# A fused attention and rational feed-forward kernel: first loads per head, a stored 1e-9 beside each row sum, and a new table of due times

## The chip, the cores and the metric

The kernel runs on one core of a Trainium2 chip. The metric is the device time of one execution in microseconds (us). TensorE (PE) multiplies matrices, VectorE (DVE), ScalarE (ACT) and GpSimd (POOL) work elementwise, and SyncE (SP) issues every DMA. Each engine runs its own instructions in the order in which the program lists them and waits, at the head of its queue, for what the next one needs.

## The reference, cut to what matters

```python
def rotate(x):                      # q, k: (4, 8, 576, 64); cos, sin by position
    x1, x2 = x[..., :half], x[..., half:]
    return np.concatenate([x1 * cos - x2 * sin, x1 * sin + x2 * cos], axis=-1)
scores = scale * np.matmul(rotate(q), rotate(k).transpose(0, 1, 3, 2))
attn = np.exp(scores - scores.max(-1, keepdims=True))
attn = attn / (np.sum(attn, axis=-1, keepdims=True) + 1e-09)
x = np.matmul(attn, v)              # then (2304 tokens, 512)
h = x @ w_in                        # 512 -> 2048
P = a[0] + a[1] * h + a[2] * h**2 + a[3] * h**3
Q = 1.0 + np.abs(b[0]) * np.abs(h) + np.abs(b[1]) * h**2
out = (P / (Q + 1e-6)) @ w_out      # 2048 -> 512
```

## The kernel before

The 32 heads are taken as 16 pairs (0 to 15). Every fp32 operand of a product is split into a high and a low half that TensorE takes as fp32r, so a product is two or three matmuls.

A pair goes through named steps, and the names are used below with the pair's number. `ld` loads q and k of both heads, each with a copy whose halves are swapped, so that the rotation is two products with a table (`ro0`, `ro1`) and a sum (`ro2`). `hi` and `lo` split the result, `kh`, `kl`, `qh`, `ql` move halves between partitions by DMA. `s0` to `s8` are nine blocks of 128 rows of scores (PSUM, two buffers), `m` their negated maxima (tiles `nm`), `x` the exponentials (tiles `e`), with the row sum written by the same instruction into `sum`. `tA`, `tB`, `tL`, `tJ` transpose e on TensorE (three PSUM buffers), `h..` and `l..` split that into `eh` and `el`, `av0` to `av3` multiply by v, `ac` and `aa` add the two halves of that (tiles `xt`, `xo`). `n0` makes 1/(sum + 1e-9) in the tile `rs`: a tensor_scalar that adds 1e-9 (L468), then a reciprocal (L469). `n1` to `n4` spread it over partitions by way of DRAM, and `f0`, `f1` scale and store the pair's rows. `vh` and `vl` split v.

POOL does `ro0`, `ro1`, `ro2`, `lo`, `vl` and `f0` of a pair. For pairs 0 and 1 the rotation and `lo` are on DVE (`rope_first`, `split_first`, and `SECOND`), because POOL's are slower. Pair 0 is loaded in four pieces (`load_first`), and its rotation has its own instructions per head.

The feed-forward part goes through 73 units, most of them 512 tokens by 128 columns of the hidden layer: `up` (tile `h`, 12 matmuls), a chain of 13 elementwise steps on ACT, DVE and POOL (`t` to `gl`; `u`, `v`, `p`, `gh`, `gl` are its tiles), and `down` (tiles `acc0` to `acc3`). Each of the 32 weight tiles comes as raw 64-bit numbers and is made fp32 by four steps `wn0` to `wn3` (ACT or POOL, then three on DVE: tiles `rawi`, `rawo`), then split by `whh` (ACT) and `whl` (POOL). `up` and `down` of a tile wait for its `whl`.

No loop writes the program's order. `Program.order` is a list scheduler at build time: it holds each step's engine, a planned duration and a due time, and at each point an engine takes, of the steps that could start soonest, the one with the earliest due time. Due times come from tables: `SLOTS` for a pair, tables of their own for pairs 0, 1, 14 and 15, multiples of `TURN`, and `DUE`, `DUE_0`, `DUE_1` for the rest. A step marked `shared` is planned not to overlap POOL's; `n0` is not marked.

```python
    def norm(self, p, i):
        if i == 0:
            rs = st["rs"] = self.p2.tile([P, NBLK], F32, tag="rs", name=f"rs{p}")
            nc.vector.tensor_scalar(rs, st["sum"], 1e-9, None, ALU.add)
            nc.vector.reciprocal(rs, rs)
```

Of the kernel before, what the change touches and what calls it, by code (L numbers as in the profile page):

```python
# [17 lines left out]
P = 128  # L18
# [13 lines left out]
def fp(ap):  # L32
    return ap.bitcast(F32)
# [16 lines left out]
}  # L50
SLOTS_14 = {
# [12 lines left out]
}  # L64
SLOTS_15 = {
# [12 lines left out]
}  # L78
SLOTS_1 = {
# [12 lines left out]
}  # L92
SLOTS_0 = {
# [1041 lines left out]
```

## Time and profile before

| | |
|---|---|
| three runs, median | 750.04 us (746.74 to 753.43) |
| the profiled execution | 749.95 us, of which 748.1 us is its span, first to last instruction |
| busy in the span | PE 92%, PE weight load 79%, DVE 81%, ACT 79%, POOL 60% |
| granted TensorE clock, mean | 0.974 of full |
| moved by DMA | 86.34 MB, 115 GB/s |

The span has five parts. Until about 44 us pair 0 is loaded, rotated and scored. From there to about 274 us the pairs follow each other, with the score block `s4` of a pair at 104.16 us and that of the next at 120.96 us. From 274 to 387 us the last two pairs and the first units of the feed-forward part are mixed. From 387 to about 735 us PE hardly idles, and the last 13 us finish the last unit. The share of an engine over the whole span mixes these parts, so the rows by stage say more. A busy PE is a PE with some matmul under way: its records overlap, so the step from one start to the next is what a matmul costs.

### The profile page before, as it was taken

To read this page: it belongs to the slowest core of one execution; us is meant where nothing else is said; L and a number is where in the kernel's file an instruction comes from. 1 tells how busy PE (TensorE), PEld (TensorE's weight loads), DVE (VectorE), ACT (ScalarE), POOL (GpSimd) and SP (SyncE) were. 2 spreads that over 40 slices of the span, in tenths; PEclk is the share of its full clock that TensorE was granted. 3 is DMA by queue.
4 is the path that set the end of the run, shared out by engine and by line. 5 is a ranking of instruction groups with operands and counts; after the bars stand their busy time and mean duration, and the time that the engine had idled before them with its cause. 6 is when DMAs were issued, how large, how long until landed. Compare 5 with 4: busy or idle time off the path is not lost.

```text
span 748.1 us, 11378 instructions
## 1 busy us (share of the span) xinstructions
PE 690.4 (92%) x3864; PEld 591.0 (79%) x3864; DVE 602.7 (81%) x941; ACT 588.5 (79%) x1110; POOL 449.5 (60%) x293
## 2 busy tenths in 40 slices
PE   5679999999999987688799999999999999999998
PEld 2668999998998976666587788888888888888986
DVE  4867999999999888989988999866866666666675
ACT  1468999999998977787878998877767777677774
POOL 0576788788887646368667676656544454444422
PEclk9599999999999999998899999999999999999999
DMA  9476676777775754363432425205200001000100
GB/s 234 132 197 164 177 201 178 192 191 199 199 209 153 190 149 154 122 186 110 170 111 85 141 85 197 72 1 169 91 1 1 0 8 56 1 1 0 43 15 29
DMA packets 35305, 86.34 MB, mean 115 GB/s; under 512 B 5024, under 2 KB 8240, under 8 KB 33328
## 3 DMA queue, kind: packets, MB, share of 16 engines
q1 hardware_dynamic: 35248, 85.62, 39.8%
q8 instruction: 31, 0.51, 0.3%
q14 instruction: 26, 0.21, 0.1%
HBM read 55.25 MB, written 12.66 MB: 91 GB/s over the span
## 4 chain that ended last, share of the span: by engine, by line
PE 73%; DVE 11%; DMA 5%; ACT 5%; issue 2%; POOL 2%; SPq 1%; POOLq 0%; ACTq 0%; DVEq 0%
PE h L810 25%; PE acc L860 9%; PE acc L859 9%; PE acc L858 9%; PE s L445 9%; PE av L533 7%; DVE nm L453 3%; PE t_B L503 2%; PE t_A L503 2%; DVE rs L468 2%; DMA q<-q 2%; ACT e L460 2%; ACT eh L520 1%; DVE el L522 1%; DMA x<-in_qk_dram 1%
## 5 line engine op out<-in xcount | busy, mean ns | idle before, releaser
L834 POOL TENSOR_TENSOR v<-v,t 128x512 f32<-128x512 f32 x68 | 88.5, 1301 | 98.0 <-ACT v L832 97.0
L445 PE MATMUL s<-ks,q 128*128 128x288 f32 (+2 forms) x672 | 121.1, 313 | 19.8 <-ACT e L460 11.7
L843 POOL TENSOR_TENSOR gl<-u,gh 128x512 fp32r<-128x512 f32 (+1 forms) x73 | 94.3, 1292 | 62.4 <-ACT gh L842 45.6
L460 ACT ACTIVATE e<-s,nm 128x576 f32<-128x576 f32 x144 | 106.4, 740 | 28.4 <-DVE nm L453 26.5
L445 PEld LDWEIGHTS s<-ks,q 128*128 128x128 f32 x672 | 98.9, 198 | 28.1 <-ACT e L460 17.7
L453 DVE TENSOR_REDUCE nm<-s 128x1 f32<-128x576 f32 x144 | 105.4, 746 | 16.7 <-PE s L445 12.8
L533 PE MATMUL av<-eh,vv 128*128 128x288 f32 x320 | 91.6, 310 | 7.5 <-DVE xo L550 7.5
L860 PE MATMUL acc<-woh,gl 128*128 128x512 f32 x234 | 92.4, 395 | 0.7 <-POOL gl L843 0.7
L858 PE MATMUL acc<-woh,gh 128*128 128x512 f32 x234 | 92.4, 395 | 0.3 <-ACT gh L842 0.3
L859 PE MATMUL acc<-wol,gh 128*128 128x512 f32 x234 | 92.4, 395 | 0.0
L533 PE MATMUL av<-el,vv 128*128 128x288 f32 x320 | 87.4, 297 | 0.2 <-DVE el L522 0.2
L831 ACT ACTIVATE t<-h 128x512 f32<-128x512 f32 (+1 forms) x73 | 43.2, 591 | 54.3 <-PE h L810 54.1
L835 DVE TENSOR_TENSOR u<-u,h 128x512 f32<-128x512 f32 (+1 forms) x73 | 49.5, 678 | 44.5 <-ACT u L833 44.4
L371 POOL TENSOR_TENSOR x<-x,tab 128x1152 f32<-128x1152 f32 x28 | 75.5, 2698 | 14.1 <-DMA x<-in_qk_dram 14.1
L839 DVE SCALAR_TENSOR_TENSOR v<-v,p 128x512 f32<-128x512 f32 (+1 forms) x73 | 49.5, 678 | 34.5 <-ACT p L838 32.2
L810 PE MATMUL h<-xh,wih 128*128 128x512 f32 (+1 forms) x204 | 75.1, 368 | 0.0
L810 PE MATMUL h<-xh,wil 128*128 128x512 f32 (+1 forms) x204 | 74.9, 367 | 0.0
L810 PE MATMUL h<-xl,wih 128*128 128x512 f32 (+1 forms) x204 | 74.7, 366 | 0.0
L533 PEld LDWEIGHTS av<-eh,vv 128*128 128x128 f32 x320 | 60.9, 190 | 9.8 <-DVE xo L550 6.9
L533 PEld LDWEIGHTS av<-el,vv 128*128 128x128 f32 x320 | 61.1, 191 | 0.4 <-DVE el L522 0.4
L832 ACT ACTIVATE v<-t,const 128x512 f32<-128x512 f32 (+1 forms) x73 | 59.1, 810 | 2.4 <-DVE p L840 0.5
L842 ACT ACTIVATE gh<-u 128x512 fp32r<-128x512 f32 (+1 forms) x73 | 45.4, 622 | 19.6 <-PE acc L859 16.9
(113 smaller groups left out, 1747.6 us busy)
## 6 DMA issues: line engine op xcount, KB each, us to landing
x<-in_qk_dram SPq DMA_DIRECT2D x15, 1152.0 KB, 7.9
ks<-q SPq DMA_DIRECT2D x30, 288.0 KB, 3.6
q<-q SPq DMA_DIRECT2D x30, 288.0 KB, 7.1
rawi<-in_w_in_dram SPq DMA_DIRECT2D x16, 512.0 KB, 4.0
rawo<-in_w_out_dram SPq DMA_DIRECT2D x16, 512.0 KB, 3.2
vf<-in_v_dram SPq DMA_DIRECT2D x16, 320.0 KB, 3.6
rb<-rd SPq DMA_DIRECT2D x32, 144.0 KB, 3.4
xd<-xo SPq DMA_DIRECT2D x16, 288.0 KB, 2.7
```

The lines of the kernel that those rows point to most:

```text
L371: eng.tensor_tensor(x[:, i], x[:, i], t, ALU.mult)
L445: nc.tensor.matmul(ps[:, half, x:x + k.shape[-1]], q, k, start=(i == 0), stop=(i == len(ops) - 1))
L453: self.nc.vector.tensor_reduce(nm, st["s", c][:, :, :HALF], AX.XY, ALU.max, negate=True)
L460: self.nc.scalar.activation(e.rearrange("p (a b) -> p a b", a=2), st["s", c][:, :, :HALF], AF.Exp, bias=st["nm", c], scale=1.0, accum_out= ...
L533: nc.tensor.matmul(po[:, :HALF], v, e, start=(i == 0), stop=(i == len(ops) - 1))
L810: self.nc.tensor.matmul(ph[:, i * n:(i + 1) * n], w[:, k * P:(k + 1) * P], x[:, :n], start=(j == 0), stop=(j == len(terms) - 1))
L832: "v": lambda: act(new("v"), d["t"], AF.Identity, bias=self.b[0], scale=self.b[1]),
L834: "w": lambda: (nc.gpsimd.tensor_tensor if u < POOL_W else tt)(d["v"], d["v"], d["t"], ALU.mult),
L843: "gl": lambda: (nc.gpsimd.tensor_tensor(new("gl", F32R), d["u"], fp(d["gh"]), ALU.subtract), self.g.update({u: (d["gh"], d["gl"])})),
L858: nc.tensor.matmul(acc, gh[:, c], hi, start=(first and i == 0), stop=False)
L859: nc.tensor.matmul(acc, gh[:, c], lo, start=False, stop=False)
L860: nc.tensor.matmul(acc, gl[:, c], hi, start=False, stop=(last and i == len(fs) - 1))
```

## The change

Four things change.

1. In DRAM and in SBUF a head's plain and swapped halves lie side by side: `np.stack([xt, sw], 3)` in place of `2`. `load_first` then reads one unbroken stretch for a head, twice as long as each of the two before, with the same number of DMAs and bytes. The rotation of the other pairs takes `x[:, :, i]` in place of `x[:, i]`: the same number of elements.
2. The table of cosines and sines comes in one DMA in place of two halves, and `ro0` of pair 0 waits for all of it.
3. The row sums live in two fixed tiles of 9 pairs of numbers, whose second numbers are 1e-9, written once. `n0` is now a tensor_reduce over each pair of numbers, in place of the tensor_scalar; the reciprocal stays.
4. All due times are new, with a few planned durations (`vh`, `x`, `ac`, `aa`). Every engine's order changes.

```diff
+        self.sums = [self.p3.tile([P, NBLK, 2], F32, tag=f"sum{i}", bufs=1, name=f"sum{i}") for i in range(2)]
+        for t in self.sums:
+            nc.gpsimd.memset(t, 1e-9)
...
-            self.nc.sync.dma_start(self.x0[r:r + D, 2 * k:2 * k + 2, h], self.qk[0][k * D:(k + 1) * D, :, h])
+            self.nc.sync.dma_start(self.x0[r:r + D, 2 * k + h], self.qk[0][k * D:(k + 1) * D, h])
...
-        self.nc.sync.dma_start(self.tab[:, i], self.tab_dram[:, i])
+        self.nc.sync.dma_start(self.tab, self.tab_dram)
...
-            bias=st["nm", c], scale=1.0, accum_out=st["sum"][:, c:c + 1])
+            bias=st["nm", c], scale=1.0, accum_out=st["sum"][:, c, :1])
...
-            nc.vector.tensor_scalar(rs, st["sum"], 1e-9, None, ALU.add)
+            nc.vector.tensor_reduce(rs, st["sum"], AX.X, ALU.add)
             nc.vector.reciprocal(rs, rs)
...
-TURN = 17.89
+TURN = 16.49
...
-    "down": 20.59, "flush": -44.65, "late": -4.20, "each": 1.75, "x": 339.04, "x0": -596.98, "wl": 489.52,
+    "flush": 39.75, "late": -57.11, "each": 2.71, "x": 158.07, "x0": -650.32, "wl": 152.63, "wn": 175.59,
...
-        return np.stack([xt, sw], 2)
+        return np.stack([xt, sw], 3)
```

Three places show what the new due times do on DVE. A row gives the line, the operation, the tile written and the tiles read; a tile's first number is its pair, or its weight tile.

The first is the start of the program on DVE. x0 and x1 are q and k of pairs 0 and 1, q20 and q21 their split forms, nm0_1 the first maximum. Before:

```order
L378 TENSOR_TENSOR x0_110<-x0_110,tab_95 128x576 x2
L380 TENSOR_TENSOR x0_110<-x0_110 128x576
L378 TENSOR_TENSOR x0_110<-x0_110,tab_95 128x576 x4
L380 TENSOR_TENSOR x0_110<-x0_110 128x576 x2
L396 TENSOR_TENSOR q20_99<-x0_110,q20_99 128x576 x2
L394 SCALAR_TENSOR_TENSOR ks0_147<-x0_110,ks0_147 64x576
L378 TENSOR_TENSOR x0_110<-x0_110,tab_95 128x576 x2
L453 TENSOR_REDUCE nm0_1_203<-s0_1_192 128x1
```

The same engine and place with the change:

```order
L379 TENSOR_TENSOR x1_119<-x1_119,tab_95 128x2x576 x2
L381 TENSOR_TENSOR x1_119<-x1_119 128x2x576
L386 TENSOR_TENSOR x0_114<-x0_114,tab_95 128x576 x2
L417 TENSOR_TENSOR q21_100<-x1_119,q21_100 128x2x576
L388 TENSOR_TENSOR x0_114<-x0_114 128x576
L386 TENSOR_TENSOR x0_114<-x0_114,tab_95 128x576 x3
L388 TENSOR_TENSOR x0_114<-x0_114 128x576
L386 TENSOR_TENSOR x0_114<-x0_114,tab_95 128x576
L388 TENSOR_TENSOR x0_114<-x0_114 128x576
L404 TENSOR_TENSOR q20_99<-x0_114,q20_99 128x576
```

Pair 1's four instructions, which stood between the maxima of pair 0, now stand ahead of most of pair 0's. Behind the last row shown come four more on x0 and ks0 and then nm0_1. Up to the first maximum of pair 1, nm1_1, the order before has six `el0` and `el4_0` rows (five of 512 columns, one of 64), the new one two of 512. SP issues the load of x1 first, then the table, then the eight pieces of x0; before it issued x1 after all of x0.

The second is the place of `n0` in the middle, here of pair 8, on DVE. xo7 and el8 are outputs of pair 7 and split transposes of pair 8, nm9 the maxima of pair 9. Before:

```order
L453 TENSOR_REDUCE nm9_1_2301<-s9_1_2286 128x1
L453 TENSOR_REDUCE nm9_3_2310<-s9_3_2296 128x1
L550 TENSOR_TENSOR xo7_2183<-av7_2_2268,xt7_2_2308 64x288
L468 TENSOR_SCALAR rs8_2328<-sum8_2071 128x9
L469 RECIPROCAL rs8_2328<-rs8_2328 128x9
L453 TENSOR_REDUCE nm9_2_2349<-s9_2_2331 128x1
L522 TENSOR_TENSOR el8_2198<-t8_B_1_2303,eh8_2196 128x512
```

With the change:

```order
L530 TENSOR_TENSOR el8_2184<-t8_A_0_2248,eh8_2182 128x512
L476 TENSOR_REDUCE rs8_2286<-sum0_107 128x9
L477 RECIPROCAL rs8_2286<-rs8_2286 128x9
L461 TENSOR_REDUCE nm9_1_2296<-s9_1_2281 128x1
L530 TENSOR_TENSOR el8_2184<-t8_A_1_2258,eh8_2182 128x512
L558 TENSOR_TENSOR xo7_2199<-av7_2_2265,xt7_2_2289 64x288
L461 TENSOR_REDUCE nm9_3_2320<-s9_3_2291 128x1
```

The division stands four rows earlier, ahead of pair 9's first maximum, and the maxima and the `el` rows alternate more. Apart from the one operation, the rows of a pair are the same in number and size.

The third is the end of the scores on DVE: the weight tiles' steps among the last maxima of pair 15. Before:

```order
L453 TENSOR_REDUCE nm15_6_4009<-s15_6_3989 128x1
L522 TENSOR_TENSOR el15_3941<-t15_A_0_3943,eh15_3939 128x512
L686 SCALAR_TENSOR_TENSOR rawi2_3806<-rawi2_3806 128x512
L690 TENSOR_SCALAR rawo0_3905<-rawo0_3905 128x512
L691 SCALAR_TENSOR_TENSOR rawo0_3905<-rawo0_3905 128x512
L550 TENSOR_TENSOR xo14_3965<-av14_2_4011,xt14_2_4039 64x288
L522 TENSOR_TENSOR el15_3941<-t15_A_1_3997,eh15_3939 128x512
L686 SCALAR_TENSOR_TENSOR rawo0_3905<-rawo0_3905 128x512
L690 TENSOR_SCALAR rawi3_4025<-rawi3_4025 128x512
L691 SCALAR_TENSOR_TENSOR rawi3_4025<-rawi3_4025 128x512
L453 TENSOR_REDUCE nm15_7_4075<-s15_7_4066 128x1
```

With the change:

```order
L461 TENSOR_REDUCE nm15_8_3989<-s15_8_3969 128x1
L530 TENSOR_TENSOR el14_3657<-t14_B_2_3940,eh14_3655 128x512
L530 TENSOR_TENSOR el15_3931<-t15_A_2_3933,eh15_3929 128x512
L558 TENSOR_TENSOR xo14_3959<-av14_1_3976,xt14_1_3994 64x288
L697 SCALAR_TENSOR_TENSOR rawi2_3807<-rawi2_3807 128x512
L692 SCALAR_TENSOR_TENSOR rawi2_3807<-rawi2_3807 128x512
L461 TENSOR_REDUCE nm15_7_4030<-s15_7_4011 128x1
```

The steps of rawo0 and rawi3 move behind the last maximum. Counted on DVE from pair 14's maximum nm14_4 to the last step `g` of unit 4, the order before has 129 rows, 42 of them weight steps, and the new one 112, with 30. To `g` of unit 8 it is 163 (57) and 149 (45), to `g` of unit 27 303 and 301. On PE, five `up` units stand ahead of the first `down` of unit 0 in the new order, four in the old one.

More of the change, by code (lines that the diff above doesn't have):

```diff
@@ L115 @@
 DUE = {
-    "ffn": 374.36, "t": 20.70, "v": 234.46, "w": -228.61, "u1": 810.56, "u2": 217.88, "ln": -365.32,
-    "u3": 29.76, "ex": -511.21, "e": -170.92, "r": 223.55, "g": -3.82, "gh": -173.95, "gl": -268.30,
-    "down": 20.59, "flush": -44.65, "late": -4.20, "each": 1.75, "x": 339.04, "x0": -596.98, "wl": 489.52,
-    "wn": -36.51, "wh": -35.53, "w0": -79.89, "w1": 10.51, "w2": 294.91, "w3": 394.40, "w4": 464.21,
-    "w5": -759.74, "w6": 263.05, "w7": 282.47, "x1": 170.86, "x1s": 25.55,
[5 rows of a table added]
 }
 DUE_0 = {
-    "t": 265.57, "v": 583.68, "w": -379.99, "u1": 354.36, "u2": -835.24, "ln": -198.44, "u3": 379.54,
-    "ex": -271.89, "e": -448.85, "r": 170.65, "g": 263.61, "gh": 5.48, "gl": -193.04, "down": 88.90,
-    "flush": -28.37,
+    "t": -7.80, "v": 396.31, "w": -9.41, "u1": 399.03, "u2": -351.99, "ln": -346.35, "u3": 427.36,
+    "ex": -358.45, "e": -342.95, "r": -56.25, "g": 416.20, "gh": 6.97, "gl": 446.65, "down": 388.26,
+    "flush": -36.80,
 }
 DUE_1 = {
-    "roq": -285.89, "rok": 0.41, "hiq": 81.20, "hik": -107.48, "loq": -46.08, "lok": -40.44,
+    "roq": -274.70, "rok": 447.98, "hiq": 438.00, "hik": 440.39, "loq": 463.53, "lok": -305.02,
 }
@@ L263, in attention_steps @@
         st[f"m{c}"] = "D", 0.665, [f"s{c}"]
-        st[f"x{c}"] = "A", 0.717, [f"m{c}"]
+        st[f"x{c}"] = "A", 0.74, [f"m{c}"]
     of = {f"{k}{j}": list(range(4) if k == "A" else range(5, 9)) for k in "AB" for j in range(4)}
@@ L272, in attention_steps @@
         st[f"av{i}"] = "P", 1.36, ["vl"] + ["l" + g for g in of if g.startswith(kinds)]
-        st[f"ac{i}"] = "A", 0.29, [f"av{i}"]
-        st[f"aa{i}"] = "D", 0.44 if i == 3 else 0.37, [f"ac{i}"]
+        st[f"ac{i}"] = "A", 0.43, [f"av{i}"]
+        st[f"aa{i}"] = "D", 0.5 if i == 3 else 0.42, [f"ac{i}"]
     avs, scores = [f"av{i}" for i in range(4)], [f"s{c}" for c in range(NBLK)]
@@ L348, in load_first, with load_table @@
         for r in (0, D):
-            self.nc.sync.dma_start(self.x0[r:r + D, 2 * k:2 * k + 2, h], self.qk[0][k * D:(k + 1) * D, :, h])
-    def load_table(self, i):
-        self.nc.sync.dma_start(self.tab[:, i], self.tab_dram[:, i])
+            self.nc.sync.dma_start(self.x0[r:r + D, 2 * k + h], self.qk[0][k * D:(k + 1) * D, h])
+    def load_table(self):
+        self.nc.sync.dma_start(self.tab, self.tab_dram)
     def warm(self):
@@ L370, in rope @@
             t = self.tab[:, i:i + 1, :].to_broadcast([P, 2, S])
-            eng.tensor_tensor(x[:, i], x[:, i], t, ALU.mult)
+            eng.tensor_tensor(x[:, :, i], x[:, :, i], t, ALU.mult)
         else:
-            eng.tensor_tensor(x[:, 0], x[:, 0], x[:, 1], ALU.add)
+            eng.tensor_tensor(x[:, :, 0], x[:, :, 0], x[:, :, 1], ALU.add)
     def rope_first(self, k, h, i, eng):
-        x = self.x0[:, 2 * k:2 * k + 2, h]
+        x = self.x0[:, 2 * k + h]
         if i < 2:
@@ L382, in split_first @@
     def split_first(self, k, h, lo, eng):
-        nc, st, x = self.nc, self.st[0], self.x0[:, 2 * k, h]
+        nc, st, x = self.nc, self.st[0], self.x0[:, 2 * k + h, 0]
         ks, q2 = self.stacks(0)
@@ L404, in split_hi @@
     def split_hi(self, p):
-        self.nc.scalar.activation(self.stacks(p)[1][:, 0, :, :S], self.st[p]["x"][:, 0], AF.Copy)
+        self.nc.scalar.activation(self.stacks(p)[1][:, 0, :, :S], self.st[p]["x"][:, :, 0], AF.Copy)
     def split_lo(self, p, eng=None):
         q2 = self.stacks(p)[1]
-        (eng or self.nc.gpsimd).tensor_tensor(q2[:, 1, :, :S], self.st[p]["x"][:, 0], fp(q2[:, 0, :, :S]), ALU.subtract)
+        (eng or self.nc.gpsimd).tensor_tensor(q2[:, 1, :, :S], self.st[p]["x"][:, :, 0], fp(q2[:, 0, :, :S]), ALU.subtract)
     def move_k(self, p, t):
@@ L457, in exp @@
         if "sum" not in st:
-            st["sum"] = self.p2.tile([P, NBLK], F32, tag="sum", name=f"sum{p}")
+            st["sum"] = self.sums[p % 2]
         e = self.e4 if c == 4 else self.e[:, self.slot(p, c % 5), c // 5]
@@ L633, in plan_first @@
             add(("warm", i), "P", 0.216, WARM_DUE + 0.01 * i, self.warm, ["ident"], [("v", [("warm", WARM - 1)])] if i == 0 else [])
-        add(("tab", 0), "S", 0.0, -90, lambda: self.load_table(0), [], size=(1, 0.75))
+        add("tab", "S", 0.0, -90, self.load_table, [], size=(1, 1.8))
         for h in range(2):
@@ L638, in plan_first @@
                 n = "qk"[k]
-                add(("ld", 0, n, h), "S", 0.0, -89 + 4 * h + 2 * k, lambda k=k, h=h: self.load_first(k, h), size=(2, 1.5))
-                if k == h == 0:
-                    add(("tab", 1), "S", 0.0, -88.5, lambda: self.load_table(1), size=(1, 0.75))
+                add(("ld", 0, n, h), "S", 0.0, -89 + 4 * h + 2 * k, lambda k=k, h=h: self.load_first(k, h), size=(2, 2.0))
                 self.prog.shared |= {(f"ro{i}", 0, n, h) for i in range(3)} | {("lo", 0, n, h)}
@@ L644, in plan_first @@
                     add((f"ro{i}", 0, n, h), e, 0.67 * f, DUE_1[f"ro{n}"] + 0.01 * i if h else 4 * k + i - 80, lambda k=k, h=h, i=i, eng=eng: self.rope_first(k, h, i, eng),
-                        [("ro1", 0, n, h)] if i == 2 else [("ld", 0, n, h), ("tab", i)] + [("ro0", 0, n, h)] * i)
+                        [("ro1", 0, n, h)] if i == 2 else [("ld", 0, n, h), "tab"] + [("ro0", 0, n, h)] * i)
                 add(("hi", 0, n, h), "A", 0.573 + 0.1 * k, DUE_1[f"hi{n}"] if h else -80, lambda k=k, h=h: self.split_first(k, h, 0, None), [("ro2", 0, n, h)])
```

132 rows, old and new, of tables (DUE, SLOTS, SLOTS_0, SLOTS_1) are left out of this document.

## The prediction

> **What bounds the kernel now.** I read the page's totals, then the busy time by stage, then the chain that ended last, then single rows. The stages come first. Columns: stretch, its length, busy us and count for PE, PE's weight load, DVE, ACT and POOL, then granted clock, DMA share and GB/s.
>
> ```profile
> span 748.1 us, 11378 instructions
> 15.00:30.00 15.00, 7.07 (x26) 6.25 (x26) 13.55 (x18) 6.50 (x12) 2.86 (x2) 0.56 0.45 171
> 100.00:150.00 50.00, 48.34 (x375) 46.18 (x375) 48.03 (x81) 46.63 (x107) 40.26 (x19) 1.00 0.73 199
> ...
> 500.00:550.00 50.00, 50.00 (x219) 40.76 (x218) 36.76 (x55) 38.04 (x60) 29.43 (x23) 1.00 0.30 98
> ...
> 274.39:300.00 25.61, 19.53 (x144) 17.74 (x144) 19.74 (x34) 19.38 (x44) 14.16 (x10) 1.00 0.54 169
> 300.00:320.00 20.00, 14.09 (x97) 12.43 (x96) 18.09 (x34) 15.02 (x33) 7.74 (x6) 1.00 0.41 133
> 320.00:341.80 21.80, 15.37 (x81) 11.76 (x79) 18.26 (x32) 19.95 (x35) 13.07 (x11) 0.99 0.49 149
> 341.80:365.00 23.20, 23.20 (x94) 19.38 (x94) 22.00 (x32) 17.22 (x29) 17.36 (x14) 0.87 0.44 152
> 365.00:386.60 21.60, 16.63 (x63) 13.24 (x62) 19.34 (x29) 17.45 (x29) 14.88 (x12) 0.84 0.39 135
> sum 112.21, PE 88.81 PEld 74.55 DVE 97.43 ACT 89.01 POOL 67.22; mean PE 17.76 PEld 14.91 DVE 19.49 ACT 17.80 POOL 13.44
> ```
>
> The feed-forward part (500 to 550) is full on PE, so no order makes it shorter. The pairs (100 to 150) are close to full on three engines at once. At the start, and in the 112.21 us where pairs and units mix, PE idles while DVE does not: there PE has 23.4 us idle (112.21 less 88.81), DVE 14.8. So three places can move: start, pairs, mix.
>
> The chain of one pair, with start, us and what ran:
>
> ```profile
> 52.62 2.03 PE s L445 x14
> ...
> 104.16 1.16 PE s L445 x10
> ...
> 107.24 0.11 PE rt L472
> 107.35 0.44 PE t_B L503 x4
> 107.79 0.53 PE s L445 x4
> ...
> 108.76 0.22 PE t_J L503 x2
> 108.98 1.33 PE av L533 x10
> ...
> 116.49 1.65 DVE rs L468
> ...
> 120.96 1.16 PE s L445 x10
> ...
> 274.39 1.16 PE s L445 x10
> ```
>
> A pair takes 16.80 us here (104.16 to 120.96). From pair 1's `s4` at 52.62 to pair 14's at 274.39 there are 13 of them in 221.8 us, 17.06 each. One link is odd: 1.65 us for nine numbers per partition. Its rows, and what POOL did then:
>
> ```profile
> L468 DVE TENSOR_SCALAR rs<-sum x16: 165/1641/2437, 46.2 to 323.6; 128x9 f32<-128x9 f32 x16
> ...
> 132.25 2.65 POOL L409 TENSOR_TENSOR q<-x,q 128x1152 fp32r<-128x1152 f32 x1 [1.46 <-ACT q L405]
> 133.29 1.64 DVE L468 TENSOR_SCALAR rs<-sum 128x9 f32<-128x9 f32 x1
> 134.97 0.22 DVE L469 RECIPROCAL rs<-rs 128x9 f32<-128x9 f32 x1
> ```
>
> The row ends at 134.93, with POOL's at 134.90. The least of the 16 takes 0.165, the median 1.641. So this tensor_scalar waits for POOL's instruction, while the reciprocal behind it takes 0.22 although POOL has begun again.
>
> **The pairs.** `n0`'s first row becomes a tensor_reduce of 18 numbers. No row here shows a reduce out of SBUF beside POOL. If it does not wait, it costs about 0.2, like the reciprocal; if it waits, 1.64 as before. I take 0.2, because the reciprocal, its nearest row, also reads SBUF and does not wait. That frees 1.44 us of DVE per pair. It is not all gain, since what is late next stands close. PE must issue, by the chain's rows, eight score blocks of 0.53 and one of 1.16, ten sets of four transposes at 0.44, one of 0.22, four `av` of 1.33 and `rt` 0.11: 15.45 us. ACT is busy 46.63 of 50, or 15.67 us per pair, and DVE falls from 16.14 to 14.7. So the gain is at most 16.80 less 15.67, 1.13 us by ACT, or 1.35 by PE's issue. At the least it is some 0.3, when the new order turns most of it into waits of ACT for maxima. I take 0.85, three quarters of ACT's bound. Over 13 pairs that is **11 us**, bounded by 4 and 17. The rest of the order in the pairs I cost at nothing: same rows, and POOL, at 40.26 of 50, covers its own waits; if that cover is gone, the lower bound holds.
>
> The Trainium skill, page SBUF — State Buffer, section Who interferes with whom, says the same of both operations: tensor_scalar may take a port pair that is an exclusive lock against GpSimd, and tensor_reduce on trn2 never contends. The first half is what the rows show; the second no run before can show. By it the sum above stands, and without it the case of the waiting reduce below.
>
> **The start.** Rows of before:
>
> ```profile
> 7.67 0.76 DVE L378 TENSOR_TENSOR x<-x,tab 128x576 f32<-128x576 f32 x1 [6.79 <-DMA x<-in_qk_dram]
> 13.88 1.43 DVE L378 TENSOR_TENSOR x<-x,tab 128x576 f32<-128x576 f32 x2 [1.14 <-DMA x<-in_qk_dram]
> 18.95 2.29 PE L445 MATMUL s<-ks,q 128*128 128x288 f32 x8 [5.96 <-DVE ks L394]
> 21.66 1.35 DVE L371 TENSOR_TENSOR x<-x,tab 128x1152 f32<-128x1152 f32 x1
> 21.11 0.74 ACT L460 ACTIVATE e<-s,nm 128x576 f32<-128x576 f32 x1 [0.16 <-DVE nm L453]
> 22.00 1.33 PE L445 MATMUL s<-ks,q 128*128 128x288 f32 x4 [0.76 <-ACT e L460]
> 28.39 1.17 ACT L405 ACTIVATE q<-x 128x1152 fp32r<-128x1152 f32 x1 [1.33 <-DVE x L373]
> 45.55 0.76 DVE L453 TENSOR_REDUCE nm<-s 128x1 f32<-128x576 f32 x1 [2.00 <-PE s L445]
> ...
> x<-in_qk_dram SPq DMA_DIRECT2D x8, 288.0 KB, 8.1
> tab<-in_tab_dram SPq DMA_DIRECT2D x2, 288.0 KB
> ```
>
> Between 7.67 and 13.88 five pieces of 288 KB came in (half the table and four of x0): 232 KB a us. The new order loads x1 first (1152 KB, being four times 288) and then the table: 864 KB have landed by 7.67, the other 864 take 3.7, so DVE starts at 11.4. Pair 0's four heads follow every 2.5 us, from 13.9 to 21.3, each ahead of its use. DVE: three rows of 1.35 on x1 to 15.5, two of 0.72 to 16.9, x1's `lo` (ACT's 1.17 is done by then) to 18.3, twelve rows of 0.72 to 26.9, then the first maximum. Thirteen such rows later, at 36.3, it reaches nm1_1, which stood at 45.55. Four more rows of `el` are still to be done then, three such and a small one, 2.3 us, so this way the new order is 7 us ahead: it no longer idles before data and `lo` of x1 is not stretched. But PE's first scores come at 25.6 rather than 18.95, after a longer idle, and a block of scores that comes after one takes 1.33, not 0.53. With two score buffers two blocks take 1.33, the maximum's 0.76 and the exponential's 0.74, so nine take 13 us. With 3.5 sets of transposes, 0.44 stretched alike to 1.1, and pair 1's first block, nm1_1 stands at about 43.8: then the gain is nothing. I take **3 us**, between, bounded by -2 (a wait for POOL at `lo`) and 7. The longer rows in DRAM and the one table DMA I cost at nothing: the bytes are the same, and x1 covers the table.
>
> A rule speaks against the later scores: the Trainium skill, page TensorE: Matmul & The Clock Gate, Part 1, says that an idle array is throttled to half rate until it has been busy for some 3.4 us. The stage rows agree on the fall (clock 0.56 from 15 to 30). By that rule dense scores would run at full rate after 3.4 us and the gain would be near 7; by the rows, where the clock stayed low through a stretch with 7.07 us of matmuls, it is the lower figure.
>
> **The mix.** The rows of DVE's weight steps (busy, then mean ns), two of PE's waits from 265 to 400, and all from 400 on (us in total, times, longest):
>
> ```profile
> L690 DVE TENSOR_SCALAR rawo<-rawo 128x512 int32<-128x512 int32 x16 | 10.5, 658 | 0.0
> L691 DVE SCALAR_TENSOR_TENSOR rawi<-wpi,rawi 128x512 int32<-128x512 int32 x12 | 8.3, 692 | 0.9
> ...
> PE av L533 <- DVE xo L550: 6.9, 6, 2.4
> PE h L810 <- DVE u L836: 5.6, 2, 5.0
> ...
> PE acc L860 <- POOL gl L843: 0.7, 1, 0.7
> PE acc L858 <- ACT gh L842: 0.3, 1, 0.3
> ```
>
> What PE waits for is DVE, twice over. To `g` of unit 8, near the end of this stretch, the new order has 14 fewer DVE rows, 12 of them weight steps. At 0.65 from start to start (0.69 less an overlap of about 0.04) they are 9.1 us. DVE is busy 97.43 of 112.21, so I let the whole come out of the stretch: **9 us**. The most is near 20, when PE's 23.4 idle us all but go and the clock (0.87 and 0.84) does not fall; the least -3, when other waits take their place. The steps come later, in units where PE is full and DVE at 36.76 of 50 has room. That cover hides them; where a tile comes after its unit it would cost up to 6 us, three tiles' steps.
>
> **Sum.** 749.95 (the profiled execution: the span and 1.85 around it) less 3, 11 and 9 is 726.95, so **727 us**. The median of the runs shown is 750.04, the same within 0.1.
>
> **The rivals.**
>
> The reduce waits like the tensor_scalar (the change then doesn't do what it says). For it: both read SBUF while POOL does; against it: the reciprocal. The 11 go: 749.95 less 12, 738.
>
> The new order gives it back. All three engines of a pair are above 46 of 50, and an order made for planned durations may meet other ones. At 0.3 us in a pair, and nothing at start and mix, it is 746.
>
> Weights come too late, which makes it slower than before. Twelve tiles' DVE steps stand later against the units, and PE waits for a tile in order. A tile's DVE steps take 2.04 us (0.66 and twice 0.69). If each of the 24 later tiles holds PE by three quarters of that, 1.5 us, that is 36, and 727 becomes 763. It decides from 1.3 us a tile (24 times 1.27 is the 23 gained and 1% more). Against it: PE lost 1.0 us to all waits after 400 (0.7 and 0.3), and nearly all `whl` rows stand more than a unit ahead.
>
> **How the numbers follow.** Forecast 0.72, the waiting reduce 0.07, given back 0.13, late weights 0.08. About 1% is what a measurement tells here, 742.5 to 757.5. The first two are faster, with a little of the third: faster 0.80, within 0.12, slower 0.08. The bounds of the terms, not all at one end, give 712 to 742 for the forecast; with part of the third case the range is 712 to 745.
>
> **What would show it.** L476 near 0.2 us in all 16; from `s4` to `s4` about 16 us; nm1_1 near 42; PE's idle time between `s4` of pair 14 and unit 9 down by 9 or more, and its clock full there; PE at 50 of 50 from 500 on. The forecast is wrong if L476 takes over 1 us, if ACT or PE waits in a pair grow by what DVE gained, or if `h` or `acc` wait for weights.

## The result, and the profile after

The changed kernel takes **720.37 us** (median of 4 runs, 719.73 to 722.84) against 750.49 for the kernel before in the same comparison (4 runs, 746.74 to 753.43): a ratio of 0.9607, 95% interval 0.9558 to 0.9656. The forecast was 727, in a range of 712 to 745. Medians and ranges below are of all runs, ratios and intervals leave out the runs of a slower state. The kernel before spreads: in three later comparisons its 17 to 29 runs had medians of 751.1 to 752.6. The profiled execution of the kernel with the new start alone is the longest of its 12 (760.51 against a median of 750.03), and only its first 65 us are read.

The profiled execution took 719.73 us, by the page:

```profile
span 718.0 us, 11373 instructions
```

The busy time by stage of the changed kernel, in the columns of the prediction (stretch, length, busy us of PE, its weight load, DVE, ACT and POOL, granted clock, DMA share, GB/s):

```profile
15.00:30.00 15.00, 5.93 (x21) 5.24 (x22) 12.58 (x18) 6.00 (x13) 4.38 (x3) 0.59 1.01 282
30.00:50.00 20.00, 18.26 (x131) 16.46 (x131) 16.34 (x28) 18.08 (x44) 14.43 (x6) 0.97 0.42 104
100.00:150.00 50.00, 48.46 (x380) 46.76 (x379) 44.76 (x83) 46.67 (x110) 40.78 (x19) 1.00 0.80 196
263.00:291.00 28.00, 24.84 (x183) 22.50 (x182) 25.91 (x46) 25.92 (x62) 16.88 (x12) 1.00 0.59 185
...
500.00:550.00 50.00, 50.00 (x219) 40.78 (x218) 34.71 (x50) 35.94 (x56) 23.86 (x19) 1.00 0.10 33
```

And two such rows of the kernel before, for the stretches that answer to the second and the fourth:

```profile
30.00:50.00 20.00, 14.71 (x77) 13.07 (x77) 14.31 (x20) 11.70 (x27) 16.51 (x6) 0.73 0.68 163
...
276.00:315.00 39.00, 27.79 (x202) 24.89 (x200) 32.15 (x56) 30.18 (x67) 17.33 (x13) 1.00 0.48 156
```

The feed-forward part is as full as it was. In the pairs PE is no fuller (48.46 of 50, before 48.34), although DVE has lost 3.27 us of work there. The start is denser from 30 us on, and what took 39 us around pair 15's maxima takes 28.

To place the gain, the rows of DVE were matched, line by line and in order, with the tiles that the program writes in that order. This gives the end of each event, in us. `nmP_B` is the maximum of block B of pair P, `u8` the last `u` of unit 8.

```
event      before   changed   lead        stretch that ends here   before   changed
nm1_1       46.30     38.15    8.2
nm2_4       71.52     63.59    7.9        start                     71.5      63.6
nm14_4     276.34    263.62   12.7        pairs                    204.8     200.0
nm15_7     315.04    291.61   23.4        mix, last two pairs       38.7      28.0
u8         392.20    361.90   30.3        mix, first units          77.2      70.3
last u     739.96    709.89   30.1        the rest                 347.8     348.0
```

So 7.9 us come from the start (forecast 3), 4.8 from the pairs (11), and 17.6 from the mix (9): 10.7 up to the last maximum and 6.9 behind it. Each number is of one execution. Two variants below have the changed kernel's order on every engine up to nm14_4, and in their traces the pairs take 202.4 and 202.2 us, not 200.0: 2 us in the pairs is what one execution differs from the next. Where a variant is named below, its numbers in such events are from its own trace in the same way.

### The profile page after: what moved, and what is told of

It reads as the page before. It is cut to its first block, busy times and chain, and to the rows that moved or that the text cites. A ratio compares the mean times of both kernels' runs of the same rounds, so it can differ in the third digit from the quotient of the medians.

```text
span 718.0 us, 11373 instructions
## 1 busy us (share of the span) xinstructions
PE 680.2 (95%) x3864; PEld 586.6 (82%) x3864; DVE 578.5 (81%) x941; ACT 584.9 (81%) x1110; POOL 447.8 (62%) x295
## 4 chain that ended last, share of the span: by engine, by line
PE 72%; DMA 14%; ACT 5%; DVE 5%; issue 1%; POOL 1%; SPq 1%; DVEq 0%; POOLq 0%; ACTq 0%
PE h L816 26%; PE acc L866 9%; PE acc L865 9%; PE acc L864 9%; PE s L453 7%; DMA ks<-q 7%; PE av L541 6%; DMA q<-q 4%; PE t_B L511 3%; ACT e L468 2%; PE t_A L511 2%; DMA const<-in_b_dram 1%; ACT eh L528 1%; PE t_J L511 1%; DMA tab<-in_tab_dram 1%
## 5 line engine op out<-in xcount | busy, mean ns | idle before, releaser
L461 DVE TENSOR_REDUCE nm<-s 128x1 f32<-128x576 f32 x144 | 107.9, 752 | 24.5 <-PE s L453 22.3
L453 PEld LDWEIGHTS s<-ks,q 128*128 128x128 f32 x672 | 97.0, 194 | 30.1 <-ACT e L468 11.2
```

The lines of the kernel that those rows point to most:

```text
L453: nc.tensor.matmul(ps[:, half, x:x + k.shape[-1]], q, k, start=(i == 0), stop=(i == len(ops) - 1))
L461: self.nc.vector.tensor_reduce(nm, st["s", c][:, :, :HALF], AX.XY, ALU.max, negate=True)
```

## The experiments

**The row sums, each way round.** One kernel is the changed one with the old row:

```diff
...
-            nc.vector.tensor_reduce(rs, st["sum"], AX.X, ALU.add)
+            nc.vector.tensor_scalar(rs, st["sum"], 1e-9, None, ALU.add)
```

> The changed kernel with n0's tensor_scalar and its own sum tile put back; order, loads and table stay. Theory A (the freed DVE time was not what the pairs of the new order gained, since q's copies by DMA set their step, 16.9 us before and after): the row takes about 1.6 us again in most pairs, DVE takes it out of its slack, and the kernel loses 2 to 8 us, 722 to 728. Rival B (the reduce is worth its 1.4 us in every pair): 13 times 1.3, 17 us, so 737.

The other is the kernel before with the new row and its fixed tiles:

```diff
...
-            nc.vector.tensor_scalar(rs, st["sum"], 1e-9, None, ALU.add)
+            nc.vector.tensor_reduce(rs, st["sum"], AX.X, ALU.add)
```

> The kernel before with only n0's tensor_reduce and the stored 1e-9; order, loads and table of before. Theory A (in the old order PE waited in the pairs for DVE and ACT and hardly for DMA): the row takes 0.16 us and the pairs fall from 16.8 towards 16.3, 4 to 8 us in all, 742 to 746. Rival B (other waits take its place at once): under 2 us, 748 to 750. Rival C (worth 0.85 a pair as the prediction had it): 739.

The first took 723.91 us (723.32 to 724.91; 0.9615 of before, 0.956 to 0.9669), the second 755.26 (751.67 to 760.46; 1.0035, 0.9997 to 1.0073). So in the new order the row is worth 3.5 us by the medians, but only 0.6 by the two ratios to the kernel before, whose intervals cover each other: a worth clear of noise is not shown. In the old order it is worth nothing that can be told; the second kernel came out above all three of its ranges, nearest to rival B. The row's durations (ns, least, median, most) in the changed kernel:

```profile
L476 DVE TENSOR_REDUCE rs<-sum x16: 150/153/174, 41.0 to 292.9; 128x9 f32<-128x18 f32 x16
```

The same row in the old order, in the second kernel:

```profile
L471 DVE TENSOR_REDUCE rs<-sum x16: 160/173/179, 45.5 to 334.2; 128x9 f32<-128x18 f32 x16
```

The old row in the new order:

```profile
L472 DVE TENSOR_SCALAR rs<-sum x16: 151/153/2190, 40.9 to 297.3; 128x9 f32<-128x9 f32 x16
```

The reduce never waits, as forecast. The second kernel is what shows it: a POOL row runs beside 15 of its 16 reduces, in the changed kernel beside 5, and beside none from pair 2 to pair 12. For the same reason the old row mostly does not wait in its new place: its median there is 0.153 us, where it was 1.641 in the old order. In pairs 2 to 12 both rows thus take 0.15 us, and what the reduce was to bring there the new place brings by itself. So the first kernel lies in theory A's range, but not in theory A's way, which had the old row wait again in most pairs. Where POOL does run, the old row still waits, here in pair 13, where POOL's row ends at 259.13:

```profile
257.16 2.00 DVE L472 TENSOR_SCALAR rs<-sum 128x9 f32<-128x9 f32 x1 [0.28 <-ACT e L464]
```

In the old order, 1.47 us less of DVE in a pair brought nothing. The chain of the second kernel in its middle (start, us, what) and two of POOL's waits from 60 to 250 us (total, times, longest) say what took over. The chain:

```profile
185.43 2.67 POOL q L412
...
188.11 4.26 DMA ks<-q
...
192.44 9.85 DMA q<-q
...
202.43 1.17 PE s L448 x7
```

POOL's waits:

```profile
POOL x L374 <- DMA x<-in_qk_dram: 20.4, 7, 5.3
POOL x L374 <- DMA vf<-in_v_dram: 11.0, 2, 5.7
```

From POOL's `lo` to the scores lie two transfers one after the other, 4.26 us for `kl` and 9.85 for `ql`; and POOL, which makes `lo`, waits for x. A pair first fell to 16.1 us, and from pair 7 on some took 18 to 21.5 us. DVE was not the only bound; the transfers behind POOL were as near. Two limits of this reading: the profiled execution is the longest of ten (760.46 against a median of 755.26), and the same chain stands, with the old row, in the profile of the kernel with only the new layout (3.49 us and 8.65 from 242.04 on). So the transfers belong to the old order and not to the reduce; how often a usual execution meets them is open.

**Where x's load stands on SP.** In the changed kernel's pairs one wait of PE stands out. Its longest from 41 to 235 us:

```profile
PE s L453 <- DMA q<-q: 7.4, 8, 1.6
```

The longest of the kernel before, from 52 to 265:

```profile
PE t_B L503 <- DVE el L522: 4.7, 10, 1.2
PE s L445 <- ACT e L460: 4.1, 12, 1.4
PE s L445 <- DMA q<-q: 0.8, 1, 0.8
```

PE no longer waits for DVE and ACT, but for `q`. The chain that ended last, in the changed kernel, from 105 us:

```profile
110.73 0.34 SPq L352
...
111.12 8.31 DMA ks<-q
...
119.44 0.02 SPq L425
...
119.49 3.79 DMA q<-q
...
123.41 1.16 PE s L453 x7
```

SP issues the load of x (L352, 1152 KB) and right behind it `kl` (288 KB), which takes 8.31 us to land. `ql` is issued when `kl` has landed (119.49, the row behind it in the chain), and PE's scores wait for `ql`. In the old order the load of x stood behind `kl` and ahead of `qh` and `ql`. Two kernels move it in pairs 2 to 13, all else as in the changed kernel: one behind `kl`, the other behind `ql`.

```diff
+    return {("ld", p + 2): at["kl", p] + 0.5 for p in range(2, 14)}
```

> The changed kernel with one DMA moved in SP's order for pairs 2 to 13: the load of x of the pair after next stands behind the second copy to ks (kl), where before it stood, not between kh and kl. Theory A (x's 1152 KB ahead of kl make kl land after 8 us, ql waits for kl and PE for ql): kl lands in about 4 us, PE's waits for q (7.4 us) go, the pairs fall from 16.7 to about 16.2, and the kernel gains 3 to 6 us, 714 to 717. Rival B (the DMA engines, 0.8 busy, set the step whatever the order): under 1 us, 719 to 721.

```diff
+    return {("ld", p + 2): at["ql", p] + 0.5 for p in range(2, 14)}
```

> The same with the load of x behind the last copy of q (ql), so that no copy of a pair has x's load ahead of it. Theory A: PE's waits for q go as well and the time is that of the run with x behind kl or 1 us less, 713 to 716, unless x then comes too late for POOL's first product (POOL waits for x over 5 us in all). Rival B: 719 to 721.

They took 714.60 us (712.34 to 716.60; 0.949 of before, 0.9451 to 0.9528), as theory A had it, and **711.33** (710.94 to 712.64; 0.9451, 0.9414 to 0.9488), 1.7 below its range, both faster than the changed kernel, whose interval (0.9558 to 0.9656) theirs do not touch. The median time to land of `ks` and `q`, by the page's part on DMA issues, in the changed kernel:

```profile
ks<-q SPq DMA_DIRECT2D x30, 288.0 KB, 5.7
q<-q SPq DMA_DIRECT2D x30, 288.0 KB, 4.6
```

The same in the second kernel:

```profile
ks<-q SPq DMA_DIRECT2D x30, 288.0 KB, 3.6
q<-q SPq DMA_DIRECT2D x30, 288.0 KB, 3.9
```

Of PE's waits for `q`, 7.4 us in the changed kernel, this is left there from 41 to 235 us:

```profile
PE s L480 <- DMA q<-q: 1.3, 1, 1.3
```

And its busy time from 100 to 150 us, in the columns above:

```profile
100.00:150.00 50.00, 49.55 (x393) 48.21 (x392) 46.44 (x86) 47.97 (x113) 42.29 (x20) 1.00 0.75 209
```

From nm2_4 to nm14_4 it takes 194.3 us where the changed kernel takes 200.0: 16.2 a pair, against 16.7 and 17.1 before, and 11 of its 12 pairs take 16.0 to 16.1. So the place of one load on SP's queue held back 5.7 of the 11 us that the prediction had for the pairs. Another 1.9 us are won ahead of nm2_4, since the edit begins with pair 2. The Trainium skill, page DMA: Bandwidth & Descriptors, section Queues, rings and completion order, says that on each DMA engine the descriptors of one queue are consumed in ring order. The rows agree: `kl` took 8.31 us behind x's load, and the median to land of `ks` is 3.6 without it ahead. In the kernel with x behind `kl` it is q's copies that have the load ahead of them, and there their median is 6.2 and that of `ks` 3.3.

**The start.** The layout and the one table load by themselves, in the kernel before:

```diff
...
-        self.nc.sync.dma_start(self.tab[:, i], self.tab_dram[:, i])
+        self.nc.sync.dma_start(self.tab, self.tab_dram)
...
-        return np.stack([xt, sw], 2)
+        return np.stack([xt, sw], 3)
```

> The kernel before with only the new layout: x of a head holds its plain and swapped half side by side, each first load is one unbroken piece of rows, and the table comes in one load. The order of the steps is the old one. Theory A (the layout is worth nothing, the gain at the start is the new order's): within 2 us of before, table and x landed no earlier than in before (7.67 and 6.79+ us after the start), nm1_1 at 45.5 +- 1. Rival B (longer rows in DRAM make the loads quicker): nm1_1 2 to 4 us earlier and the kernel 2 to 4 us faster, with the first loads landing sooner after their issue than 8.1 us.

It took 757.00 us (746.67 to 762.17; 1.0031, 0.9988 to 1.0074), no difference that can be told; nm1_1 stood at 45.86. The 7 us that its profiled execution lies behind arise at pairs 11 to 14, not at the start. Then the kernel before with the first loads and DVE's first rows in the new order, and pair 1's copies earlier on SP:

```diff
...
+    to = {("ld", 1): -1.0, ("tab", 0): -0.9, ("tab", 1): -0.8, ("lo", 1): second + 0.5}
+    to.update({(n, 1): first - 0.5 + 0.1 * i for i, n in enumerate(("ro0", "ro1", "ro2", "hi"))})
...
```

> The kernel before with only the start in the new order: x of pair 1 loaded first, its rotation and split ahead of pair 0's on VectorE, and its copies into the stacks earlier on SyncE. Layout, row sums and all later places are the old ones. Theory A (the place of pair 1's rotation makes the start shorter, and what is won there stays): nm1_1 at 38 to 40 us (before 45.55), nm2_4 7 to 8 us earlier than 71.52, the kernel 6 to 8 us faster (742 to 744). Rival B (the pairs of the old order give it back, since x of the pairs after comes no earlier): nm2_4 5 us or more earlier, but nm14_4 less than 2 us earlier than 276.3, and the kernel within 2 us of before.

It took 751.49 us (747.26 to 764.88; 0.9984, 0.9945 to 1.0022), with nm1_1 at 46.23. Neither theory had this: the lead did not even arise. PE's rows there, with the wait of each in brackets:

```profile
40.09 0.63 PE L535 MATMUL t_A<-ident,e 128*128 128x128 f32 x4 [0.78 <-DVE el L554]
...
42.32 0.97 PE L535 MATMUL t_J<-ident,e 128*128 128x128 f32 x4 [1.07 <-DVE el L554]
44.27 0.63 PE L535 MATMUL t_L<-ident,e 128*128 128x128 f32 x4 [0.98 <-DVE el L554]
44.65 0.79 PE L477 MATMUL s<-ks,q 128*128 128x288 f32 x4
```

The same place in the changed kernel:

```profile
35.50 0.81 PE L453 MATMUL s<-ks,q 128*128 128x288 f32 x4 [0.84 <-ACT e L468]
36.14 0.60 PE L511 MATMUL t_A<-ident,e 128*128 128x128 f32 x4
36.50 0.78 PE L453 MATMUL s<-ks,q 128*128 128x288 f32 x4
37.12 0.60 PE L511 MATMUL t_A<-ident,e 128*128 128x128 f32 x4
38.20 0.80 PE L453 MATMUL s<-ks,q 128*128 128x288 f32 x4 [0.49 <-ACT e L468]
```

With PE's old order, pair 1's first block (44.65) stands behind transposes of pair 0 that wait one after another for `el`; in the changed kernel it stands at 36.50, among them. The block itself waits for nothing at 44.65, and SP had issued pair 1's last copy of q by 22.54 there. So a third kernel takes the whole new order, on all engines, up to pair 2's `m4`, and the old one from there:

```diff
+    head = new[:new.index(("m4", 2)) + 1]
+    return head + [n for n in order if n not in set(head)]
```

> The kernel before (its layout, its tensor_scalar row), with the changed kernel's order on all engines up to pair 2's maximum m4 and its own from there on. Before, nm1_1 stood at 46.3 and nm2_4 at 71.5; in the changed kernel at 38.2 and 63.6; moving VectorE's and SyncE's rows alone had left nm1_1 at 46.2. Theory A (what shortens the start is that TensorE takes pair 1's scores between pair 0's transposes): nm1_1 at 38 to 40, nm2_4 at 63 to 66, and the kernel 5 to 8 us faster (743 to 746). Rival B (the old order of the pairs gives the lead back, waiting for x): nm2_4 as in A, but nm14_4 within 2 us of 276.3, and the kernel within 2 us of before.

nm1_1 came to 39.14 and nm2_4 to 64.50, as theory A had it, but the kernel took 750.03 us (744.39 to 760.51; 0.9958, 0.992 to 0.9995). A lead of 7 us ends as 3, between theory A and rival B. So the new order makes the start without the new layout. That it is PE's part of the order is read from the rows above: this kernel moves ACT's and POOL's rows too. Half of the lead or more is given back behind nm2_4; where, and whether by waiting for x as rival B had it, is not shown, as the one trace is of the longest execution. In the changed kernel, and in the one with only the row put back, nm2_4's lead of 7.9 us stands at 12.7 and 10.1 by nm14_4.

**The pairs alone.** The kernel before with the new order only between those two places:

```diff
+    mid = [n for n in new[:new.index(("m4", 14)) + 1] if n not in set(head)]
+    return head + mid + [n for n in order if n not in set(head + mid)]
```

> The kernel before (its layout, its tensor_scalar row), with the changed kernel's order between pair 2's maximum m4 and pair 14's, and its own start and end. From nm2_4 to nm14_4 before took 204.8 us, the changed kernel 200.0, and the changed kernel with the old row 202.7. Theory A (the new order of the pairs is hardly better in itself, since q's copy comes late behind x's load): 202 to 204 us, the kernel 0 to 3 us faster. Rival B (the new order of the pairs is worth what the changed kernel shows and more with a shorter start taken away): under 201 us, and the kernel 4 us or more faster.

It took 749.18 us (747.07 to 752.21; 0.9982, 0.9956 to 1.0008), and 205.9 us from nm2_4 to nm14_4, a little over what theory A named; its conclusion holds. Five of the 12 pairs take 16.0 to 16.1 us, the others 16.9 to 19.8. Alone, the new order of the pairs is worth nothing that can be told.

**The mix.** First the changed kernel with six weight rows put back ahead of pair 15's last maximum:

```diff
+    last = at["m7", 15]
+    steps = [(f"wn{i}", *w) for w in (("o", 0), ("i", 3)) for i in range(4)]
+    return {n: last - 0.9 + 0.1 * i for i, n in enumerate(steps)}
```

> The changed kernel with two weight tiles' rounding steps (six VectorE rows and their first steps) put ahead of pair 15's last maximum, where the old order has them. Theory A (in the mix every VectorE row costs its length, some 0.65 us): nm15_7 at 295 to 296 us instead of 291.6, and the kernel 3 to 4 us slower (724). Rival B (VectorE has room there): nm15_7 within 1 us, and the kernel within 1 us of the changed one.

It took 728.32 us (727.04 to 731.48; 0.9664, 0.9623 to 0.9705): 8 over the changed kernel by the medians, more than theory A, and 4 by the two ratios. Its profiled execution is the longest of its six (731.48). Up to nm14_4, where the order is the changed kernel's row for row on every engine, it was already 4.1 us late, with 10.0 us of PE's waits for `q` against 7.4; this part is not the edit's, and why those transfers took longer in that comparison stays open. From nm14_4 to the last `u` it takes 453.9 us, the changed kernel 446.3: the edit costs 7.6 in this execution, or 1.3 us a row, twice a row's own length; by the ratios it would be 0.7. DVE at that place:

```profile
299.10 1.66 DVE L721 SCALAR_TENSOR_TENSOR rawi<-rawi 128x512 int32<-128x512 int32 x1
300.68 0.74 DVE L490 TENSOR_REDUCE nm<-s 128x1 f32<-128x576 f32 x1
301.35 0.21 DVE L559 TENSOR_TENSOR el<-t_J,eh 128x64 fp32r<-128x64 f32 x1
```

PE behind it:

```profile
301.70 1.08 PE L540 MATMUL t_A<-ident,e 128*128 128x128 f32 x4 [4.95 <-DVE el L559]
```

PE stands still for 4.95 us, because `el` of pair 15 is queued behind the weight rows, and when it goes on its four transposes take 1.08 us instead of 0.60, at a granted clock of 0.50 from 301.70 to 305.00. Then all weight steps from there on, 80 places earlier in the order:

```diff
+    return {n: i - 80 for n, i in at.items() if n[0] in ("wl", "wn0", "wn1", "wn2", "wn3", "whh", "whl")
+            and i > at["m7", 15]}
```

> The changed kernel with all steps of the weight tiles (loads, rounding, splits) from pair 15's last maximum on 80 places earlier in the order, which gives 41 weight rows on VectorE up to unit 4 and 55 up to unit 8 (the changed kernel 30 and 45, before 42 and 57). Theory A (the mix is shorter because weight rows left it, at 0.65 us each): u8 6 to 7 us later than 361.9 and the kernel 6 to 7 us slower (727). Rival B (the mix is shorter because of the order of the pairs' own steps and the units' steps, not of the number of weight rows): u8 within 2 us, the kernel within 2 us of the changed one.

It took 753.67 us (750.08 to 756.22; 1.0017, 0.9988 to 1.0046): all of the change's gain is lost, far more than either theory had. The edit put 19 weight rows between nm14_4 and nm15_7, where the kernel before has 14 and the changed one 9, and DVE reached some before their data:

```profile
301.10 0.43 DVE L724 TENSOR_SCALAR rawi<-rawi 128x512 int32<-128x512 int32 x1 [2.87 <-DMA rawi<-in_w_in_dram]
307.69 0.43 DVE L724 TENSOR_SCALAR rawo<-rawo 128x512 int32<-128x512 int32 x1 [2.02 <-DMA rawo<-in_w_out_dram]
```

PE waited 12.78 us for `el` there:

```profile
313.11 1.09 PE L539 MATMUL t_A<-ident,e 128*128 128x128 f32 x4 [12.78 <-DVE el L558]
```

So this kernel does not weigh the old order, but it shows what a weight row ahead of its data costs. The chain of the kernel before has the same link in small, just ahead of its last maximum:

```profile
308.21 4.67 DMA rawi<-in_w_in_dram
312.96 0.69 ACT rawi L681
313.68 0.70 DVE rawi L691
314.37 0.67 DVE nm L453
```

The fair test is the kernel before with the new order from pair 14's `m4` on:

```diff
+    head = order[:order.index(("m4", 14)) + 1]
+    return head + [order[i] for i in OTHER if order[i] not in set(head)]
```

> The kernel before (its layout, its tensor_scalar row), with its own order up to pair 14's maximum m4 and the changed kernel's order from there on. In before 463.6 us lie between nm14_4 and the last u, in the changed kernel 446.3. Theory A (the last two pairs and the first units are shorter by their order alone, mainly because 9 instead of 14 weight rows stand ahead of pair 15's last maximum): 446 to 448 us from nm14_4 to the last u, the kernel 15 to 18 us faster (733 to 735). Rival B (the gain there needs what the new start and pairs leave behind, loads that are further on): half of it or less, 742 or more.

It took 735.56 us (734.03 to 749.50; 0.9784, 0.9743 to 0.9826), half a microsecond over theory A's range, with 447.9 us from nm14_4 to the last `u`, within it. The mix stands by itself, whatever came ahead of it.

**A version beyond both.** In the kernel with x behind `ql`, PE waits 6.2 us in two places for `xo` of pair 15. The next kernel moves those rows ahead of the units':

```diff
...
+        to["ac%d" % i, 15] = at["av%d" % i, 15] + 0.5
+        to["aa%d" % i, 15] = at["av%d" % i, 15] + 0.6
...
```

> The changed kernel with x's load behind q's second copy in pairs 2 to 13 (that alone took 711.3), and with pair 15's last three copies of av on ScalarE and their sums xo on VectorE right behind their matmuls, ahead of the units' rows. There the trace showed TensorE waiting 6.2 us in two places for xo. Theory A (those two waits lie on the path that sets the end): 706 to 708. Rival B (the units' rows that are then later delay the next unit by as much): 710 to 712.

It took 713.54 us (711.70 to 714.59; 0.9491, 0.9458 to 0.9524): no gain, as rival B had it, and 1.5 over its range. PE's longest wait from 284 to 325 us, in the kernel without the move:

```profile
PE av L568 <- DVE xo L585: 6.2, 2, 3.7
```

Its longest two in the kernel with it:

```profile
PE h L847 <- DVE u L873: 5.9, 2, 4.6
PE av L572 <- DVE xo L589: 1.0, 1, 1.0
```

The wait for `xo` became one for `u` of almost the same length. Both are waits for DVE; this move only changed who waits for it. The kernel with x behind `ql`, at 711.33, stays the best that was run.

## Why the prediction was right in the sum and wrong in its terms

**The total**, 727, was 6.6 us above the result, with the sign and the range right. That the sum is this near is luck: one term was over twice too large and two were about half of what came or less, and these cancel.

**The pairs** (11 forecast, 4.8 measured, lower bound 4) failed at the sentence that the rest of the order in the pairs costs nothing. It looked at DVE, ACT and PE, and took from the profile that POOL covers its own waits. The step that was right is the reduce's duration: 0.150 to 0.179 us in 32 places, and the Trainium skill's page SBUF — State Buffer, section Who interferes with whom, by which a tensor_reduce on trn2 never contends, agrees. But the 1.44 us of DVE that it was to free are freed in pairs 2 to 12 by the new place as well, with the old row. What was wrong is what is late next: not a maximum or an exponential, but `ql`, behind `kl`, behind x. The changed kernel shows it as 7.4 us of waits, and moving x gives 5.7 us back, which makes the pairs' gain 10.5. The figure of 0.85 a pair was thus near what the engines allow, and the queue that was left out of the sum took half of it. How much of the 4.8 is the reduce's stays open. The kernel with the old row takes 202.7 us from nm2_4 to nm14_4, the changed one 200.0, and 1.6 of that arise in the last pair, beside the 2.00 us of the old row shown above; but the two traces with the reduce and the same order up to there take 202.4 and 202.2. The rest is the order together with the new start, since alone it brings nothing.

**The start** (3 forecast, bound 7, measured 7.9) failed at two steps. One is the rate of the first loads, taken as 232 KB a us. DVE's first row on data in the changed kernel:

```profile
8.12 2.63 DVE L379 TENSOR_TENSOR x<-x,tab 128x1152 f32<-128x1152 f32 x2 [7.24 <-DMA tab<-in_tab_dram]
```

PE's first scores there:

```profile
21.86 2.29 PE L453 MATMUL s<-ks,q 128*128 128x288 f32 x8 [8.48 <-DVE ks L402]
```

x1 and the whole table were there at 8.12 us, not 11.4, and the scores came at 21.86, not 25.6: the whole chain behind the loads moved by the 3.3 to 3.7 us that were mis-sized. The rate was not the same for all loads: from 4 to 6 us, with x1's load issued first, the DMA engines moved 412 GB/s, where the kernel before moved 218. The layout is not what did it: the kernel with the old layout and x1 loaded first had both at 6.71 us. The other is the low clock, which the prediction carried on to nm1_1. Two short rows of the changed kernel, in the columns of the prediction:

```profile
28.00:30.00 2.00, 2.00 (x9) 2.00 (x9) 0.76 (x1) 0.44 (x3) 2.00 (x2) 0.50 1.05 184
32.00:34.00 2.00, 1.79 (x13) 1.39 (x12) 0.88 (x3) 1.96 (x6) 1.92 (x2) 1.00 0.11 34
```

The clock was 0.50 from 28 to 30 us and 1.00 from 32 to 34, four ahead of nm1_1; from 30 to 50 it was 0.97, where the kernel before had 0.73. The Trainium skill, page TensorE: Matmul & The Clock Gate, Part 1, has sustained work release the throttle after some 3.4 us; the fuller stretch and its 0.97 agree, with PE busy without a gap from 27.68 to 32.72 as the clock rises. The prediction weighed that rule and set it aside for "the lower figure". What the prediction had not named is that the lead needs the order of more engines than DVE: the kernel with DVE's and SP's part alone has none, and its rows point to PE's.

**The mix** (9 forecast, up to 20; measured 17.6) was right in place and in the wait (PE for DVE), and mis-sized: 0.65 us for a row that leaves was the price of DVE's time alone. A weight row ahead of the last maximum cost up to 1.3 us, since PE stands still behind `el` and restarts slowly, and one that is reached before its load costs the load. Of the 17.6 us, 16 came with the new order of this stretch alone. How these divide between weight rows and the other rows that moved was not told apart, so that the weight rows are the main cause is argued, not shown.

**The rivals.** The reduce does not wait. "The new order gives it back" was half true, in the pairs alone, through a transfer rather than a maximum. Late weights did not come: from 362 us on PE waits 0.2 us in all for other engines. That the order would be worth as much as it is in the mix was in the range, but not in the sum.

**Parts and whole.** By their ratios, the start alone saves 3 us, the pairs 1, the mix 16, and the reduce and the layout nothing: about 20 of 30. The other 10 need more than one part; as each of these savings is known to 2 to 4 us, the 10 may be 4 or 15. A likely reason is that an earlier start, or a freer DVE, shows in the time only where the pairs do not wait for transfers. No kernel with just two of the three orders was run, so this is not shown.

## What to carry to other kernels

Where three engines are close to full, a freed engine is worth what the next resource lets through, and the queue that issues the DMAs is one of these resources: follow a pair's small copies through SP's order, and see which large load stands ahead of them. A row of side work ahead of a chain's last link can cost more than its own length: the idle time of the engine that waits, and the lateness of its own load. Test parts of a new schedule by splicing the two orders, and run some of them together too, since parts that gain nothing alone can gain together. Before an operation is changed because it waits beside another engine's row, see whether moving it does the same.

## What the runs showed of the hardware that was not expected

- The same tensor_scalar of 9 numbers takes 0.153 us or over 2, by where it stands against POOL's rows: in all traces together it took over 0.2 us 77 times, and each of these began while a POOL row was under way and ended within 0.05 us of that row's end. The reduce of 18 numbers took 0.150 to 0.179 in all 32 places of two orders, 20 of them beside a POOL row.
- A scalar_tensor_tensor of 512 columns on 32-bit integers, usually 0.69 us, took up to 1.82 where both operands were in SBUF, and 0.68 to 0.70 in all 48 places of the changed kernel where one was in PSUM. All 69 long ones in the traces began while a POOL row was under way and ended 0.55 us behind it.
- A copy of 288 KB landed in 8.31 us behind a load of 1152 KB on the same queue, and in 3.6 in the median without it. At the start the DMA engines, at a share of 0.99 in both kernels, moved 412 GB/s from 4 to 6 us with x1's load first, and 218 before.
